# Pairing 64-row matmuls on both row halves in a fused linear-attention and gated-MLP block, with a constant in the rows for z2's shift

## The chip, the cores and the metric

One core of a Trainium2 chip runs the whole kernel. The metric is the time of one execution on the device in microseconds (us). The profiled execution also has a span, from its first to its last recorded instruction.

## The reference

All inputs are bf16; S = 2048 tokens, D = 448 features, 16 heads of 28, F/2 = 896. Part A is a linear attention with softmax features, part B a gated MLP whose gate mixes tokens. Both work on a layer norm whose scale and shift come from a condition c.

```python
mod = (silu(c) @ w_mod).reshape(1, 6, 1, 448)          # sa, ca, ga, sb, cb, gb
h = layernorm(x) * (1 + ca) + sa
q, k, v = split_heads(h @ wqkv)                        # 16 heads of 28
phi_q = concat(softmax(q @ w_phi), softmax(-(q @ w_phi)))   # phi_k likewise
o = (phi_q @ (phi_k.T @ v)) / (phi_q @ sum(phi_k) + 1e-6)
x = x + ga * (o @ wo)
h = layernorm(x) * (1 + cb) + sb
z = gelu(h @ w_in)                                     # 448 -> 1792
z1, z2 = z[..., :896], layernorm(z[..., 896:])
g = w_sp @ z2 + b_sp[:, None]                          # 2048 x 2048 over tokens
x = x + gb * ((z1 * g) @ w_out)
```

## The kernel before

The tokens lie in 16 tiles of 128. Features are cut into four chunks of 112 rows (448 = 4 x 112), each in its own slot of 128 rows, so a product over the 448 features is four matmuls of 112 rows accumulated in one PSUM bank. The layer norm's shift rides on row 113 of the first chunk: xpad holds ones behind each chunk's 112 columns (m1, L676), the transposes put them into row 112 of hT, and the weight has the shift's product there; hence KR = [113, 112, 112, 112] (L847). The scale of the norm is multiplied into the weight rows (SC, L776; SCw, L782).

The order of every engine's work is one table written out by hand, ORDER (L482). Each word is a step: its name, its arguments, after @ the PSUM slot (A0, A1, A2 are pairs of banks, B0 and B1 single banks), after / the engine (V VectorE or DVE, S ScalarE or ACT, G GpSimd or POOL, Y SyncE or SP). The steps are issued in the order of the table, so each engine runs its own steps in that order; waits between engines follow from the data and from the reuse of slots. DMA loads and transposes stand in the table too, nearly all in SP's queue (T1 and T2 through turn, L832; T3, L1007; W, L1048, which brings the token-mixing matrix transposed into four 512-column pieces, of which the last three reuse the memory of Eq and hT; ld, the loads of L639; oD, L1077).

The stages, in the order of the table:

1. Start: the condition's silu (ct, ce), loads, folding w_phi into the q and k weights (FT, ET, PF, EP, L789 to L815), the columns of shift and scale (colform, L743; col_shift, col_scale), the shift rows of q, k, v (SH, L758) and the scalings (SC). Dummy matmuls du keep TensorE at work meanwhile. The first norm is l1s, l1e, l1r, l1a; its first four tiles are transposed by TensorE (X, XE), the others by DMA (T1).
2. The k and v stage: per tile kM, kE/kF (two exponentials), kS, kR, kP, vM, vC, and kA, the sum over tokens. Half of the q units (qM:0 to 2) lie among them.
3. The numerator stage: KV and KZ build the block-diagonal matrix; qM makes the rest of the q features (each 8 matmuls of 512 columns, with two exponentials qE/qF on ACT); per tile nM (8 matmuls of 120 columns), nX (ACT copies the sums), nC, per two tiles nS (three small DVE operations: add, reciprocal, multiply, L948), nT (DVE, 896 wide), nA (adds the two halves into opad), T2 (transposes to oT), wM or wN (L966: four matmuls with the output projection; wN adds x by an identity matmul), wR (new x and its sum, ACT or DVE), wQ (its squares), l2R, l2r, l2a (second norm into xpad), T3 (transposes to hT). The shift rows of w_in are SHw (L763: four units of four matmuls of 448 columns), its scalings SCw.
4. The z stage: per tile zM (L1011: 8 matmuls of 448 columns into both banks of an A slot), zG (gelu with its sum), zQ (squares), zR and zW (moments), zN (the norm into z2n). z1 is made transposed: yM (L1040) is one of 7 x 4 units of four matmuls of 512 columns into one bank, of any slot, yG its gelu.
5. The g stage: gM (L1055: 16 matmuls over all tokens), gG (two DVE operations), oM (seven matmuls), oE, oD. Some z1 units lie among the gM here.

The core of the two products and of the output projection:

```python
def zM(i, slot):
    t = ps["z" + str(i)] = bank(slot, "z2_ps")
    for hf in range(2):
        for m in range(KC):
            nc.tensor.matmul(t[:, hf, 0:D], lhsT=hT[0:KR[m], i, m, :], rhs=win_s[0:KR[m], m, FH + hf * D:FH + (hf + 1) * D], ...)
```

The second path (general_path) runs only if a sum overflows, and does not run here; guard (L1080) is the test for it, with a one-column matmul.

Of the kernel before, what the change touches and what calls it, by code (L numbers as in the profile page):

```python
# [481 lines left out]
ORDER = """  # L482
m3 m4 m1/G m2b/V m2a/V ld:x0/Y l1s:0 ld:c/S ld:wq/S du:3@A2 ct@B0 tbl ce:1 ce:2 l1e:0,1/G l1r:0,1 l1a:0/G ce:3 ce:4 du:14@A2 FTq:0@B1 du:1@A2 FTq:1@B0
ETq:0/S X:0@A2 XE:0/S ld:wk/Y FTk:1@A1 ETk:1/S FTk:0@B1 ETk:0/S ld:phi/Y ETq:1/V bd/V scb ld:x1/Y l1s:1 l1e:1,2/G l1r:1,2 l1a:1/G PFq:3@B0 PFq:2@A2
PFq:1@A1 EPq:2/S EPq:1/S ld:x2/Y EPq:3/V l1s:2 l1s:3 l1e:2,4/G l1r:2,4 du:4@A0 PFk:0@B0 PFk:2@B1 PFq:0@A2 PFk:1@A0 ld:wsa/Y du:1@A1 csA@A1 EPk:0/S
EPk:1/S PFk:3@B0 X:1@A0 EPk:3/S XE:1/S EPk:2/S EPq:0/V esA SHq@A2 ld:wca/Y ccA@B0 l1a:3/V X:3@A1 l1a:2/V ecA SCq:0/V SCq:3/V SCq:2/V SCq:1/V X:2@A0
SHk@B0 XE:3/S XE:2/S ld:wv/Y ld:x3/Y SCk:0/S ld:x4/Y SHv@B1 SCk:2/V SCk:1/V SCv:2/V SCv:3/V l1s:4 l1s:5 l1s:6 l1s:7 l1s:8 l1s:9 l1s:10 ld:wmgb/Y
ld:x5/Y ld:wo/Y ld:wmga/Y SCv:1/S SCv:0/S l1e:4,8/G l1r:4,8 l1a:5/G l1a:4/G SCk:3/S qM:0@A2 vM:0@B0 qF:0 vC:0 qE:0 kM:0@B1 vM:1@A1 vC:1 kE:0 kM:1@B0
vM:2@A2 vM:3@A1 l1a:6/G l1a:7/G kF:0 kF:1 kE:1 vC:2 kM:2@B1 kM:3@B0 kS:0 l1s:11 kS:1 kR:0 l1e:8,12/G l1r:8,12 kP:0/V kR:1 kP:1/G l1a:9/G vC:3 kE:2
qM:1@A2 gr:1@A1 kF:3 kE:3 kF:2 ge:1 qE:1 T1:4,6 kA:0@A0 gr:0@B0 kM:4@B1 qF:1 kF:4 kE:4 kS:2 kS:3 kR:2 l1s:12 T1:6,8 ld:wout/Y qM:2@A1 kA:1@A0 kM:5@B1  # L490
kR:3 kP:2/V l1a:8/G kP:3/G kS:4 l1s:13 kR:4 kP:4/V T1:8,10 W:0,2 W:0,5 l1a:10/G wts:4/G l1a:11/G T1:10,12 ge:0 ld:wsb/S qF:2 kA:2@A0 vM:4@B0 kA:3@A0
kE:5 kF:5 kM:6@B1 l1s:14 l1s:15 l1e:12,16/G l1r:12,16 l1a:13/G vC:4 qE:2 kE:6 kF:6 kA:4@A0 vM:5@B0 kM:7@A2 kM:8@B1 vM:6@A1 kE:7 vC:5 kF:7 kS:5 kR:5
l1a:15/G l1a:14/G kP:5/V kS:6 kS:7 kR:6 kR:7 kP:6/V kP:7/V l1a:12/G T1:12,14 wos:0/G ld:win1/S kF:8 T1:14,16 W:0,0 W:0,1 ld:wcb/Y W:0,7 ld:bsp/Y W:0,4
vC:6 kA:5@A0 vM:7@B0 kM:9@A2 vM:8@A1 kE:8 kF:9 vC:7 kE:9 kA:6@A0 kM:10@B1 kE:10 kF:10 vC:8 kA:7@A0 kM:11@B0 vM:9@A2 kM:12@B1 kF:11 kE:11 W:0,3
ld:win0/Y vC:9 kS:8 kR:8 kS:9 kR:9 kP:8/G kS:10 kS:11 kR:10 kP:9/G kR:11 kP:10/V kP:11/G kA:8@A0 kE:12 kF:12 vM:10@B0 kM:13@A2 vC:10 kA:9@A0 kF:13
kE:13 kS:12 kR:12 kP:12/G kS:13 kR:13 kP:13/G vM:11@B0 vC:11 kA:10@A0 kM:14@B1 kE:14 kF:14 wts:0/G wos:1/G wts:6/G wos:2/G wts:2/G wts:1/G wos:3/G
kA:11@A0 kS:14 kR:14 kP:14/V vM:12@B0 kM:15@A2 vC:12 kF:15 kE:15 vM:13@B1 vC:13 kA:12@A0 kS:15 kR:15 kP:15/V vM:14@B0 kA:13@A0 vM:15@B1 vC:14 vC:15
kA:14@A0 csB@B0 kA:15@A0 esB KV:0/V KV:1/V KZ:0 KZ:1 qM:3@A2 ccB@B0 nM:0@A1 nM:1@A0 ecB qF:3 nX:0 SHw:3@B0 SHw:2@B1 nX:1 nC:0 nC:1 nS:0 nT:0 nA:0/V
T2:0,1 W:0,6 nT:1 SCw:3,1/G SCw:1,1/G SCw:0,2/V SCw:0,3/V SCw:2,1/V nA:1/G T2:1,2 qE:3 qM:4@A2 qM:5@A1 qF:4 qE:4 nM:2@A0 nM:3@A2 nX:2 nC:2 nX:3 nC:3
nS:1 qF:5 nT:2 nT:3 qE:5 wN:0@B0 wR:0/S SHw:1@B1 dm:9,3 nM:4@A1 nM:5@A0 SCw:0,1/S nX:4 nX:5 nC:4 nC:5 nS:2 nA:2/G nT:4 nA:3/G nT:5 nA:4/G wN:1@B0  # L500
wQ:0/S wR:1/S wQ:1/S SHw:0@B1 SCw:2,0/S l2R:0,2/G l2r:0,2 l2a:0/G SCw:0,0/V nA:5/V T2:2,4 T2:4,6 qM:6@A2 nM:6@A1 nM:7@A0 wN:2@B0 wN:3@B1 qE:6 nX:6
nC:6 nX:7 nC:7 nS:3 nT:6 nT:7 qF:6 wR:2/S wQ:2/S wR:3/S wQ:3/V l2R:2,4/V nA:6/G nA:7/G l2r:2,4 l2a:3/G l2a:2/G qM:7@A2 nM:8@A1 nM:9@A0 wN:4@B0 wM:5@B1
W:1,1 T3:0,1 T2:6,8 qE:7 nX:9 nC:9 nX:8 qF:7 zM:0@A2 wR:4/S gt zG:0 nC:8 l2a:1/V nS:4 nT:8 nT:9 T3:1,2 wR:5/V nM:10@A1 nX:10 wM:6@B0 wQ:4/V wR:6/V
SCw:1,0/G SCw:3,0/G wQ:5/S l2R:4,6/G l2r:4,6 l2a:4/G nM:11@A0 nX:11 nC:10 nC:11 zQ:0/S zM:1@A2 zG:1 zQ:1/S zR:0,2/G zW:0,2 nA:8/V nS:5 nA:9/V nT:10
T3:2,4 wM:7@B0 wR:7/V l2a:5/V W:1,5 T2:8,10 T3:4,6 yM:0,0@B1 zM:2@A2 zM:3@A1 yG:0,0 wQ:6/S zG:2 zG:3 nT:11 nM:12@A0 nM:13@A2 wQ:7/V zN:0/V zN:1/V
nX:12 wM:8@B0 wM:9@B1 nC:12 nX:13 nC:13 zQ:3/S zQ:2/S zM:4@A1 nA:10/V nS:6 wR:8/V nA:11/G nT:12 nT:13 wR:9/V nA:12/V nA:13/V l2R:6,8/G l2r:6,8 l2a:6/G
l2a:7/G T2:10,12 wQ:8/S wQ:9/V zR:2,4/G zW:2,4 yM:0,1@B0 l2R:8,10/G l2r:8,10 l2a:8/G l2a:9/G zG:4 yG:0,1 zQ:4/S zN:2/V zN:3/V zM:5@A0 nM:14@A2
nM:15@A1 wN:10@B0 wN:11@B1 zG:5 nX:14 nX:15 nC:14 nC:15 nS:7 wR:10/S wQ:10/V nT:14 nT:15 nA:14/V nA:15/V wR:11/S zQ:5/S zR:4,6/G zW:4,6 T3:6,8 zM:6@A0
zG:6 wQ:11/S zQ:6/S T2:12,14 W:1,0 wM:12@B0 wM:13@B1 zM:7@A2 l2R:10,12/V yM:0,4@A1 yM:1,4@A0 l2r:10,12 l2a:11/G T3:8,10 T2:14,16 zG:7 zQ:7/S zN:4/V
zN:5/V zR:6,8/G zW:6,8 wR:13/V yG:0,4 wQ:13/S zM:8@A2 zM:9@A1 l2a:10/V wR:12/V wM:14@B0 wM:15@B1 wQ:12/V l2R:12,14/V W:1,3 T3:10,12 W:2,1 l2r:12,14  # L510
l2a:12/G zN:6/V zN:7/V yG:1,4 zG:8 zG:9 zQ:8/S W:1,4 zM:10@A2 zM:11@A1 zQ:9/S zR:8,10/G zW:8,10 zG:10 zG:11 zQ:11/S wR:14/V l2a:13/V T3:12,14 W:2,3
W:2,7 wR:15/V wQ:14/V wQ:15/V l2R:14,16/V yM:1,2@B0 zM:12@A2 zM:13@A1 yG:1,2 zG:12 yM:1,3@B0 yM:0,2@B1 yM:2,1@A2 yM:2,5@A0 zQ:10/V zN:8/V zN:9/V
zR:10,12/V l2r:14,16 l2a:14/V l2a:15/V zG:13 zQ:13/S zW:10,12 T3:14,16 W:1,2 zN:10/V zN:11/V zQ:12/V W:2,0 W:2,6 W:1,7 W:2,5 W:2,4 W:2,2 yG:1,3 yG:2,1
zM:14@A1 zM:15@A2 yG:2,5 W:1,6 zG:14 zG:15 zQ:15/S yM:1,5@B0 yG:0,2 yM:3,0@A1 yM:0,6@A2 yM:1,1@A0 yG:3,0 yG:1,1 yG:1,5 wts:3/G zR:12,14/V zW:12,14
zN:12/V zN:13/G zQ:14/V yM:3,6@B1 yM:0,3@A1 yM:1,6@B0 yG:0,3 yG:1,6 yM:1,0@A0 yG:1,0 yG:3,6 yM:3,3@A1 yM:0,5@B0 yG:0,5 yG:3,3 yG:0,6 zR:14,16/V
zW:14,16 zN:14/G zN:15/V gM:0,6@B1 gM:0,3@B0 gG:0,3 gM:0,4@A2 gG:0,6 gM:0,2@B0 yM:2,4@B1 yM:2,6@A1 yG:2,6 yG:2,4 gG:0,4 gG:0,2 yM:3,5@A2 yM:3,1@B0
yM:2,3@B1 yG:3,5 wts:5/V yG:2,3 yG:3,1 gM:0,0@A2 gG:0,0 gM:0,5@B0 gG:0,5 yM:2,0@B1 gM:0,1@A2 gG:0,1 gM:1,4@B0 oM:0,0,7@A2 oM:3,0,7@A1 yM:3,4@A0 gG:1,4
oE:0 oM:2,0,7@B0 yM:3,2@A2 yG:3,4 yG:2,0 yG:3,2 guard@A0 gM:1,5@B1 oM:1,0,7@A2 oE:1 oE:2 oE:3 gM:1,2@A0 gG:1,2 gM:1,1@B0 gM:1,3@A2 gM:1,0@A1 gG:1,3
gG:1,0 gM:1,6@A2 oD:0/Y oD:3/Y oD:2/Y gG:1,1 gG:1,5 gG:1,6 gM:2,0@B0 yM:2,2@B1 yG:2,2 W:3,0 W:3,3 W:3,7 W:3,1 W:3,6 W:3,4 W:3,2 gM:2,2@A2 gG:2,0
# [658 lines left out]
```

## Time and profile before

| what | us |
|---|---|
| median of 3 runs (264.61 to 271.07) | 265.28 |
| the profiled execution's own time | 264.1 |
| its span | 262.2 |
| PE (TensorE) busy in it | 251.1 (96%) |
| DVE busy | 158.1 (60%) |
| ACT busy | 107.4 (41%) |
| POOL busy | 89.3 (34%) |

PE is the matmuls, PEld the weight loads, which run beside them; the granted TensorE clock is 0.997 of full speed over the span. The chain that ended last is 87% PE work. A row of a group gives line, engine, operation, output<-inputs by the program's names and sizes, count, then busy time and mean duration, then the idle time ahead of it and what ended it. Matmuls overlap, so a group's pitch (start to start) is shorter than its mean duration; the chain of waits and the timeline, with starts and merged lengths, give the pitch.

### The profile page before, as it was taken

What the parts mean: (1) busy time and instruction counts of PE and PEld (TensorE: products, weight loads), DVE (VectorE), ACT (ScalarE), POOL (GpSimd) and SP (SyncE); (2) the same over time, 40 slices, a digit from 0 to 9 for tenths busy, and PEclk for the clock granted to TensorE, in tenths of its full rate; (3) what the DMA queues carried; (4) which work ended last, traced back from release to release, by engine and by line L of the source; (5) the groups of instructions that cost most, each with busy time, mean ns of one, the idle gap of its engine ahead of it and who ended that gap; (6) DMA issues with size and microseconds to landing.
All of it is one profiled execution on the core that took longest, in us unless ns stands there. A gap on an engine that the chain in (4) does not pass through costs nothing.

```text
span 262.2 us, 4353 instructions
## 1 busy us (share of the span) xinstructions
PE 251.1 (96%) x1639; PEld 135.6 (52%) x1648; DVE 158.1 (60%) x359; ACT 107.4 (41%) x222; POOL 89.3 (34%) x149
## 2 busy tenths in 40 slices
...
GB/s 187 265 287 118 215 224 207 225 159 54 66 103 126 98 118 131 171 131 173 162 0 2 1 0 0 20 2 75 0 2 143 157 0 0 20 105 2 0 38 61
DMA packets 68655, 25.23 MB, mean 96 GB/s; under 512 B 58129, under 2 KB 68498, under 8 KB 68626
## 3 DMA queue, kind: packets, MB, share of 16 engines
...
HBM read 8.87 MB, written 1.84 MB: 41 GB/s over the span
## 4 chain that ended last, share of the span: by engine, by line
PE 87%; DVE 7%; DMA 2%; issue 1%; POOL 1%; ACT 0%; ACTq 0%; DVEq 0%; POOLq 0%
PE g_ps L1059 37%; PE z_ps L1043 9%; PE z_ps L1015 9%; PE o_ps L1072 8%; PE k_ps L852 4%; PE v_ps L860 4%; PE q_ps L907 3%; PE x_ps L971 3%; DVE f_t L955 3%; PE kvacc L883 3%; DMA f_wq_raw<-in_A_wqkv_dram 2%; PE num L935 2%; PE sh_ps L761 1%; PE pf_ps L811 1%; DVE f_w L952 1%
## 5 line engine op out<-in xcount | busy, mean ns | idle before, releaser
L1059 PEld LDWEIGHTS <-f_z2n 128*128 128x128 bf16 x560 | 50.2, 98 | 46.9
L1065 DVE TENSOR_TENSOR f_gb<-g_ps,f_bsp 128x512 f32<-128x512 f32 (+2 forms) x35 | 20.4, 583 | 55.9 <-PE g_ps L1059 53.7
L1059 PE MATMUL g_ps<-f_Eq,f_z2n 128*128 128x512 bf16 x218 | 49.0, 379 | 0.3
L1046 ACT ACTIVATE f_z1T<-z_ps 128x512 bf16<-128x512 f32 x28 | 15.6, 592 | 61.8 <-PE z_ps L1043 61.7
L1015 PE MATMUL z_ps<-f_win,f_hT 112*128 112x448 bf16 (+1 forms) x128 | 26.1, 352 | 0.0
L1043 PE MATMUL z_ps<-f_hT,f_win 113*128 113x512 bf16 (+1 forms) x112 | 26.1, 379 | 0.0
L1059 PE MATMUL g_ps<-f_hT,f_z2n 128*128 128x384 bf16 (+1 forms) x224 | 25.1, 272 | 0.0
L1059 PE MATMUL g_ps<-f_wsp,f_z2n 128*128 128x512 bf16 x109 | 24.5, 379 | 0.2
L1072 PE MATMUL o_ps<-f_wout,f_z1T 128*128 128x448 bf16 x112 | 23.0, 352 | 0.1
L1075 DVE TENSOR_TENSOR f_xpad<-o_ps,f_x 128x448 bf16<-128x448 f32 x16 | 9.6, 620 | 20.7 <-PE o_ps L1072 20.7
L1066 DVE TENSOR_TENSOR f_z1T<-f_gb,f_z1T 128x512 bf16<-128x512 f32 (+2 forms) x35 | 20.5, 585 | 1.5
L1015 PEld LDWEIGHTS <-f_hT 112*128 112x128 bf16 (+1 forms) x128 | 12.4, 97 | 12.0 <-DMA f_hT<-f_xpad 0.4
L912 ACT ACTIVATE f_Eq<-q_ps 112x1024 bf16<-112x1024 f32 x16 | 16.1, 1030 | 5.6 <-PE q_ps L907 5.6
L1043 PEld LDWEIGHTS <-f_win 113*128 113x128 bf16 (+1 forms) x112 | 10.9, 97 | 13.0
L855 ACT ACTIVATE f_E<-k_ps 128x448 bf16<-128x448 f32 x32 | 15.9, 550 | 4.1 <-PE k_ps L852 2.5
L866 DVE TENSOR_REDUCE f_ksum<-f_E 128x32 f32<-128x896 bf16 x16 | 16.7, 1060 | 0.8 <-ACT f_E L855 0.8
L955 DVE TENSOR_TENSOR f_t<-num,f_w 128x896 bf16<-128x896 f32 x16 | 16.8, 1084 | 0.4
L1019 ACT ACTIVATE f_z2g<-z_ps 128x896 bf16<-128x896 f32 x16 | 14.7, 916 | 3.8 <-PE z_ps L1015 3.6
L1072 PEld LDWEIGHTS <-f_z1T 128*128 128x128 bf16 x112 | 10.9, 98 | 10.1
L907 PE MATMUL q_ps<-f_hT,f_Wq 113*128 113x512 bf16 (+1 forms) x64 | 15.2, 379 | 0.6 <-DVE f_t L955 0.6
L860 PE MATMUL v_ps<-f_wv,f_hT 113*128 113x448 bf16 (+1 forms) x64 | 14.6, 352 | 0.0
L852 PE MATMUL k_ps<-f_Wk,f_hT 113*128 113x448 bf16 (+1 forms) x64 | 14.5, 352 | 0.0
...
## 6 DMA issues: line engine op xcount, KB each, us to landing
...
```

Source lines behind the costliest of these rows:

```text
L852: nc.tensor.matmul(t[:, 0, 0:D], lhsT=hT[0:KR[m], i, m, :], rhs=Wk[0:KR[m], m, :], start=(m == 0), stop=(m == KC - 1))
L860: nc.tensor.matmul(t[:, 0, 0:D], lhsT=hT[0:KR[m], i, m, :], rhs=wv[0:KR[m], m, :], start=(m == 0), stop=(m == KC - 1))
L866: nc.vector.tensor_reduce(out=ksum[:, i], in_=Er[i % NR][:].rearrange("p s (c f h) -> p (s c) h f", c=4, h=HP), axis=AX.X, op=ALU.add)
L907: nc.tensor.matmul(t[:, u, :], lhsT=Wq[0:KR[m], m, cc * CB:cc * CB + P], rhs=hT[0:KR[m], 4 * st:4 * st + 4, m, :], start=(m == 0), stop=(m ...
L912: nc.scalar.activation(out=Eq[st // 2][0:CB, 2 * c2:2 * c2 + 2, s, (st % 2) * 512:(st % 2 + 1) * 512], in_=ps["q" + str(n)][0:CB, :, :], f ...
L955: nc.vector.tensor_tensor(out=tr[i % 2][:], in0=numv(i)[:, :, :, 0:DH], in1=wr[i // 2 % 2][:, i % 2].unsqueeze(3).to_broadcast([P, 2, H, D ...
L1015: nc.tensor.matmul(t[:, hf, 0:D], lhsT=hT[0:KR[m], i, m, :], rhs=win_s[0:KR[m], m, FH + hf * D:FH + (hf + 1) * D], start=(m == 0), stop=(m ...
L1043: nc.tensor.matmul(t[:, 0, :], lhsT=win_s[0:KR[m], m, fc * P:(fc + 1) * P], rhs=hT[0:KR[m], 4 * st:4 * st + 4, m, :], start=(m == 0), stop ...
L1059: nc.tensor.matmul(g[:, 0, 0:b - a], lhsT=later["z2n"][:, s_, fc * P:(fc + 1) * P], rhs=wspT[t][:, s_, a:b], start=(s_ == 0), stop=(s_ == ...
L1065: nc.vector.tensor_tensor(out=gb, in0=ps["G%d_%d" % (ch, fc)][:, 0, 0:b - a], in1=bsp[:, t * TCHF + a:t * TCHF + b], op=ALU.add)
L1066: nc.vector.tensor_tensor(out=z, in0=gb, in1=z, op=ALU.mult)
L1072: nc.tensor.matmul(ps["o" + str(t)][:, 0, 0:D], lhsT=later["z1T"][:, fc, t * P:(t + 1) * P], rhs=wout_s[:, fc, :], start=(fc == 0), stop=( ...
```

## The change

The rows are cut anew for w_in, the output projection and what is multiplied with them: windows of 128 rows that begin at rows 0, 128, 192 and 320. Windows 0, 1 and 3 are full; of window 2 only its upper 64 rows are used (rows 256 to 319). So 448 rows are seven halves of 64. A unit with two banks then takes, for each bank, seven 64-row matmuls; PAIRS puts them in pairs, one on the lower row half for one bank and one on the upper half for the other bank. In part one (four pairs) the lower half writes bank 0 and the upper half bank 1; in part two (three pairs) it is the other way round. Part two's first matmuls wait for a no-op on SP (zP, yP, wP), which waits for part one's last matmul. Other work of PE stands between the parts in the table.

- z2 (zM, zB) and z1 (yM, yB; now 14 units of 1024 columns in an A slot, with one gelu each) are done in pairs, and so is the output projection of tiles 8 to 15, two tiles at a time (wS, wM/wN, wB/wC). Tiles 0 to 7 keep one bank and whole matmuls (wU, wV): windows 0, 1 and 3 with 128 rows, window 2 with 64.
- The ones behind the chunks are gone from the second norm. l2a now adds a constant: x times rstd plus (mean term + 0.125), with l2t making that number per tile. z2's shift then is one row vector added to all scaled weights (SHu: 8 matmuls of 448 columns, uC, SCu: a tensor-by-tensor addition of 128 x 896); z1's shift is a bias of its gelu (SHz: 28 one-column matmuls, SBz). SHw and esB are gone, eg1, eg2 and gB are new.
- nA and l2a write 512 columns (the windows overlap) instead of 448. w_in and wo are loaded as windows in two loads each, so there are three more loads.
- nS is split into nD, nI and nS, so that other steps can stand between. dm's dummies are no longer in the table.
- The table is new throughout: at the start k's weights are folded ahead of q's, wq is loaded through SP; all z1 units stand before the first gM; zQ is 8 times on ACT (13 before), nA four times on POOL (7 before).

```diff
+SHIFT = 0.125
+PAIRS = [((0, 0, 0), (1, 1, 0)), ((0, 0, 1), (1, 1, 1)), ((0, 0, 2), (1, 1, 2)), ((0, 0, 3), (1, 1, 3)),
+         ((1, 0, 0), (0, 1, 0)), ((1, 0, 1), (0, 1, 2)), ((1, 0, 3), (0, 1, 3))]
+def wins(v):
+    return bass.AP(tensor=v.tensor, offset=v.offset, ap=[list(v.ap[0]), [192, 2], [1, 256]])
...
+m1/V m3 m4 ld:c/S m2a/V du:3@A2 ct@B0 tbl ce:1 ld:x0/Y ld:x2/Y ce:2 ce:3 ce:4 scb ld:wk/Y ld:x1/Y ld:phi/Y du:14@A2 FTk:1@B0 ETk:1/S FTk:0@B1 l1s:0
...
+nX:13 nA:10/V nC:12 nC:13 nD:6 l2t:5/V nI:6 nS:6 l2t:4/V gt wQ:6/S nA:11/G nT:12 nT:13 l2t:3/G l2a:3/G l2a:4/G l2a:5/G wS:8@B0 zM:0@A1 wM:8@B1 zP:0
+zB:0 wP:8 wB:8 wR:8/V wR:9/V nA:12/V zG:0 wQ:7/S l2R:6,8/G l2r:6,8 l2t:6/G l2t:7/G l2a:6/G zQ:0/S T2:10,12 zM:1@A0 nM:14@A1 nM:15@A2 nX:14 nX:15 nC:14
+nC:15 nA:13/V nD:7 nI:7 nS:7 nT:14 nT:15 T3:2,4 zP:1 zB:1 T3:4,6 zG:1 wQ:8/S zQ:1/S zR:0,2/G zW:0,2 wQ:9/S l2a:7/V l2R:8,10/V W:2,3 wS:10@B0 wN:10@B1
+wP:10 zM:2@A0 zP:2 wC:10 zB:2 zG:2 zM:3@A1 zM:4@A2 zM:5@A0 T2:12,14 wR:11/S wR:10/S wQ:11/S W:1,2 zP:3 zP:4 T3:6,8 zB:3 wS:12@B0 zB:4 zQ:2/V zN:0/V
...
+    def load_wins(eng, j, dst, src):
+        eng.dma_start(out=dst[:, 2 * j:2 * j + 2], in_=src[192 * j:192 * j + 256].rearrange("(k p) n -> p k n", p=P))
...
+    W4 = [0, 128, 192, 320]
+    ROWS = [slice(0, P), slice(0, P), slice(64, P), slice(0, P)]
+    HALF = [slice(0, 64), slice(64, P)]
+    def eg1(eng):
+        eng.tensor_scalar(out=tneg[:], in0=cb1[:], scalar1=-1.0 / D, scalar2=None, op0=ALU.mult)
+    def eg2():
+        nc.vector.scalar_tensor_tensor(out=g4[:], in0=ps["csB"][:, 0, 0:KC], scalar=1.0 / (D * SHIFT), in1=tneg[:], op0=ALU.mult, op1=ALU.add)
+    def gB(eng):
+        copy_on(eng, Gb[:], g4[:].unsqueeze(2).to_broadcast([P, KC, P]))
...
-    def SHw(n, slot):
-        t = ps["SHw" + str(n)] = bank(slot, "sh_ps")
+    def SHu(h, slot):
+        t = ps["SHu" + str(h)] = bank(slot, "su_ps")
         for m in range(KC):
-            nc.tensor.matmul(t[:, 0, 0:D], lhsT=Gb[0:CB, m, :], rhs=win_s[0:CB, m, n * D:(n + 1) * D], start=(m == 0), stop=(m == KC - 1))
+            nc.tensor.matmul(t[:, 0, 0:D], lhsT=Gb[ROWS[m], m, :], rhs=win_s[ROWS[m], m, FH + h * D:FH + (h + 1) * D], start=(m == 0), stop=(m == KC - 1))
+    def SCu(m, eng):
+        v = win_s[:, m, FH:2 * FH]
+        eng.tensor_tensor(out=v, in0=v, in1=ub[:].rearrange("p a d -> p (a d)"), op=ALU.add)
+    def SHz(slot):
+        t = ps["SHz"] = bank(slot, "sz_ps")
+        for fc in range(FC):
+            for m in range(KC):
+                nc.tensor.matmul(t[:, 0, fc:fc + 1], lhsT=win_s[ROWS[m], m, fc * P:(fc + 1) * P], rhs=g4[ROWS[m], m:m + 1], start=(m == 0), stop=(m == KC - 1))
...
+    def sP(key):
+        n = passed[key] = nc.sync.nop()
+        tc.add_manual_dep(n.ins, first[key].ins.name, SYNC, reason="part one of the unit")
+    def pairs(part, key, dst, lhs, rhs, extra=()):
+        steps = list(extra) + [[(bk, lhs(bk, HALF[hf], m), rhs(bk, HALF[hf], m)) for bk, hf, m in pr_] for pr_ in (PAIRS[:4] if part == 0 else PAIRS[4:])]
+        for n, st_ in enumerate(steps):
+            for bk, l, r in st_:
+                ins = nc.tensor.matmul(dst[bk], lhsT=l, rhs=r, start=(part == 0 and n == 0), stop=(part == 1 and n == len(steps) - 1))
+                if part == 0:
+                    first[key] = ins
+                elif n == 0:
+                    tc.add_manual_dep(ins.ins, passed[key].ins.name, SYNC, reason="the other row half writes this bank next")
...
-            nc.tensor.matmul(t[:, 0, 0:D], lhsT=oT[0:CB, i % 4, cc, :], rhs=wo_s[0:CB, cc, :], start=(cc == 0 and not with_x), stop=(cc == KC - 1))
+        for n, m in enumerate((0, 1, 3, 2)):
+            nc.tensor.matmul(t[:, 0, 0:D], lhsT=oT[ROWS[m], i % 4, m, :], rhs=wo_s[ROWS[m], m, :], start=(n == 0 and not with_x), stop=(n == KC - 1))
...
+    def l2t(i, eng):
+        eng.tensor_scalar(out=nt2[:, i:i + 1], in0=m2[:, i:i + 1], scalar1=v2[:, i:i + 1], scalar2=SHIFT, op0=ALU.mult, op1=ALU.add)
...
+    def zM(i, part, slot=None):
+        if part == 0:
+            ps["z" + str(i)] = bank(slot, "z2_ps")
+        t = ps["z" + str(i)]
+        pairs(part, "z%d" % i, [t[:, bk, 0:D] for bk in range(2)], lambda bk, r, m: hT[r, i, m, :], lambda bk, r, m: win_s[r, m, FH + bk * D:FH + (bk + 1) * D])
...
+    def yG(sp, fc):
+        nc.scalar.activation(out=stage_b()["z1T"][:, fc, sp * 1024:(sp + 1) * 1024], in_=ps["y%d_%d" % (sp, fc)][:].rearrange("p a d -> p (a d)"), func=ACT.Gelu_apprx_tanh,
+                             bias=zb1[:, fc:fc + 1])
```

190 lines of the change are left out of this document (104 added, 86 removed).

## The prediction, made before the changed kernel ran

> **What bounds the kernel now.** I read the page's busy times first, then the busy time by stretch, then what TensorE (PE) waited for, then the chain that ended last. The first line is the page's, the next seven are the stretches that the later steps use: the start, the k and v stage, the numerator stage up to the first z2 product, the z2 stage, the last z1 units ahead of the gate (g) products, and the two halves of the g stage.
>
> ```profile
> PE 251.1 (96%) x1639; PEld 135.6 (52%) x1648; DVE 158.1 (60%) x359; ACT 107.4 (41%) x222; POOL 89.3 (34%) x149
> ```
> ```profile
> 0.00:15.50 15.50, 12.63 (x152) 9.43 (x153) 10.03 (x37) 9.34 (x17) 7.34 (x27) 1.00 0.97 240
> 15.50:54.60 39.10, 38.73 (x306) 22.57 (x305) 36.49 (x70) 30.92 (x60) 31.78 (x33) 1.00 1.03 206
> 54.60:79.25 24.65, 22.36 (x190) 12.78 (x189) 20.83 (x48) 16.75 (x37) 15.57 (x21) 1.00 0.37 83
> 79.25:122.80 43.55, 42.97 (x256) 22.55 (x256) 37.57 (x109) 37.52 (x86) 32.58 (x68) 1.00 0.71 134
> 122.80:131.50 8.70, 8.70 (x42) 3.88 (x40) 1.84 (x7) 6.39 (x12) 2.01 (x2) 1.00 0.93 164
> 131.50:175.00 43.50, 43.29 (x202) 19.90 (x205) 13.46 (x23) 5.92 (x11) 0.00 (x0) 1.00 0.01 4
> 175.00:257.70 82.70, 82.40 (x500) 44.44 (x502) 37.24 (x68) 0.60 (x1) 0.00 (x0) 1.00 0.20 43
> ```
> ```profile
> PE num L940 <- DVE f_t L955: 1.6, 1, 1.6
> ```
>
> The columns of a stretch are its length and the busy time of PE, its weight loads, DVE, ACT and POOL, then the granted clock (1.00), the DMA share and GB/s. PE is the bound almost everywhere: from 79.25 to 257.70 it idles about 1 us in 178. Only in the numerator stage (54.60 to 79.25) it idles 24.65 - 22.36 = 2.3 us, and PE's longest wait, 1.6 us, is for DVE's f_t (nT). So a matmul taken away after 79 us is worth its pitch; one taken away before is worth it only if DVE and ACT allow it. In the z2 stage DVE and ACT are each busy 37.5 us of 43.55, 86%: little room once PE is shortened.
>
> **The change part by part.** The pitches are from the chain of waits (start, length, what).
>
> ```profile
> 56.34 0.38 PE cf_ps L747 x16
> ...
> 67.72 0.39 PE num L940 x9
> 68.11 0.85 PE num L935 x16
> 68.95 0.19 PE x_ps L969
> 69.14 0.76 PE x_ps L971 x4
> 69.91 0.76 PE sh_ps L766 x4
> 70.66 1.75 PE q_ps L907 x8
> ...
> 104.78 3.04 PE z_ps L1015 x16
> ...
> 122.81 8.68 PE z_ps L1043 x40
> ```
>
> A 512-column matmul takes 8.68/40 = 0.217 us, a 448-column one 3.04/16 = 0.190, a one-column one 0.38/16 = 0.024. If the two halves of a pair run side by side, a pair costs one pitch:
> - z1: 28 units x 4 = 112 matmuls become 14 units x 7 = 98 pairs: -14 x 0.217 = -3.0.
> - z2: 16 x 8 = 128 become 16 x 7 = 112 pairs: -16 x 0.190 = -3.0.
> - output projection of tiles 8 to 15: 32 become 28 pairs, -0.8; but the identity product runs nine times instead of seven, +0.4.
> - shift rows: 16 SHw matmuls go (-3.0), 8 SHu come (+1.5), 28 one-column SHz come (28 x 0.024 = +0.7).
> - The nine dummies of dm go: 0.39 us inside a wait for nT, so nothing.
>
> Together -7.2 us of PE work: 6.8 behind the first z2 product, where PE is the bound, and 0.4 ahead of it.
>
> **Switching between full height and half height.** SHz and SHu hold a 64-row matmul among 128-row ones for each of 7 + 2 units, wU/wV for 8 tiles (17 x 2 = 34 switches), and the pair stage is entered and left twice (4). The trace has no 64-row matmul. Its nearest row is the one-column matmul of the guard, a change of the array's shape in width.
>
> ```profile
> 169.00 1.03 PE L1043 MATMUL z_ps<-f_hT,f_win 113*128 113x512 bf16 x4
> 169.96 0.16 PE L1086 MATMUL fl_ps<-f_ones,f_flb 128*1 128x1 bf16 x1
> 170.06 1.04 PE L1059 MATMUL g_ps<-f_Eq,f_z2n 128*128 128x512 bf16 x4
> ```
> ```profile
> 169.96 0.08 PEld L1086 LDWEIGHTS <-f_flb 128*1 128x1 bf16 x1 [0.42 <-issue]
> ```
>
> The four z1 matmuls should stream 4 x 0.217 = 0.87 us, to 169.87; the guard's load starts only at 169.96, and the next full one 0.10 after it, where the pitch would be 0.024. So in and out cost (0.19 - 0.02)/2, about 0.08 us a switch. Bounds: 0, and 0.10. I take 0.08: 34 x 0.08 = 2.7 us ahead of the z2 products and 0.3 behind. [...]
>
> **The numerator stage.** From the end of the k stage (54.60) to the first z2 product PE now has five qM (5 x 1.75), fourteen nM (14 x 0.425), two colforms (0.76), SHz and SHu (2.2), and wV/wU for eight tiles (7.4): 25.0, with switches 27.7 us. DVE's chain has, per pair of tiles, from nC to the end of the second nT:
>
> ```profile
> 73.57 0.30 DVE f_cr L946 x2
> ...
> 74.83 2.09 DVE f_t L955 x2
> ```
>
> 73.57 to 76.92, 3.35 us. nM:13 needs nT:10, five and a half pairs: 18.4. DVE's other work in today's stretch is 7.4 (20.83 less the four pairs in it); six more nA and SCu:2 come, three SCw, wQ:3 and l2R:2,4 go, and I leave it at 7.4. With about 2 us until the first numerators have been drawn out that is 27.8, beside PE's own 27.7, and each waits for the other at every pair. Walking both engines' orders tile by tile with these durations I get the first z2 product 29.7 us behind the k stage: 2.0 us of PE idle, as the 2.3 now. The bounds are 27.7 and 32.0 (twice the idle). ACT nearly fills the stretch too: some 26 us, an estimate from the two ACT rows of the z stage by columns (ten qE and three scalings at about 1.0, seven wR and seven wQ at about 0.6, nX, gB, uC and the table load). POOL gets three SCu (128x896, tensor by tensor) and three SCs:
>
> ```profile
> L873 POOL TENSOR_TENSOR f_phik<-f_E,f_kr 128x896 bf16<-128x896 bf16 x7 | 11.9, 1710 | 2.6 <-PE k_ps L852 2.6
> ```
>
> At 1.7 us each at most 10.3, covered: between SHu and the first z2 product PE has some 20 us of qM, nM and wV. Without that cover it would cost up to 10.
>
> **Start.** Now k is folded first. The first full-height product behind the folding is kM:0, which waits for ACT's two SCk, behind two ETk, four EPk, four EPq and three XE.
>
> ```profile
> 8.49 1.73 ACT L799 COPY f_wTk<-tps 112x896 bf16<-112x896 bf16 x2
> 10.08 1.00 ACT L799 CAST f_Wq<-pf_ps 112x448 bf16<-112x448 f32 x2
> ```
> ```profile
> 15.48 1.90 PE L907 MATMUL q_ps<-f_hT,f_Wq 113*128 113x512 bf16 x8
> ```
>
> 1.73 + 13 x 0.5 = 8.2 us, begun when wk has landed (now about 7.2, as for wq), gives 15.4 if ACT never waits; with waits between folds and copies I take 16.3. PE now becomes dense at 15.48: +0.9. Bounds: -0.1, and +2.8 if wv, now queued behind x3 as well, holds SHv (448 KB at the 240 GB/s of the first stretch are 1.9 us more). csB moves out of the k stage, -0.4. The k stage then ends at 55.1.
>
> **The z stage.** From the first z2 product to g: z2 112 x 0.190 = 21.3, z1 98 x 0.217 = 21.3, wM 5.7, nM:14 and 15 0.85, switches 0.3: 49.4. ACT up to zG:15:
>
> ```profile
> L1019 ACT ACTIVATE f_z2g<-z_ps 128x896 bf16<-128x896 f32 x16 | 14.7, 916 | 3.8 <-PE z_ps L1015 3.6
> L983 ACT ACTIVATE f_junk<-f_z2g 128x896 bf16<-128x896 bf16 x13 | 12.4, 950 | 0.3
> ```
>
> 16 zG at 1.0 (with the accumulator's read), 8 zQ at 0.95, five yG at 1.0 (1024 wide, from 0.92 for 896), eight wQ and wR at 0.6 (448 wide): 33 us against PE's 35.6 there. PE still bounds, barely. Every two-bank unit now needs one of the three A slots, which nM:14 and 15 use too, and the z1 fillers no longer fit the single banks. I give 2.0 us of new idle, bounds 0.6 (the z2 stretch now, 43.55 - 42.97) and 2.3 (the numerator stretch); nearest the latter, since DVE and ACT are filled alike.
>
> Each unit's second part waits for a no-op on SP, queued with the transposes:
>
> ```profile
> 115.97 1.23 SPq L1009 DMA_TRANSPOSE f_hT<-f_xpad  x1
> 117.25 11.05 SPq L1051 DMA_TRANSPOSE f_Eq<-in_B_w_sp_dram  x8
> ```
> ```profile
> SPq L834 <- DVE f_opad L961: 8.0, 4, 3.3
> ```
>
> A transpose holds SP 1.23 to 1.38 us, and one may wait 3.3 us for nA. In the new table nearly every second part stands behind 0.9 to 3.6 us of other PE work, with at most two transposes ahead of its no-op (zP:3 behind T2:12,14 and W:1,2, 2.6 us, against 3.6). So 0 beyond the 2.0; upper end, 34 no-ops each behind a transpose, 34 x 1.3 = 44.
>
> **The sum.** 55.1 + 29.7 + 49.4 + 2.0 = 136.2: g starts, with no z1 unit left. Now g starts at 131.5 and PE ends at 257.70, with nine z1 units (9 x 4 x 0.217 = 7.8) between: 126.2 - 7.8 = 118.4. PE ends at 254.6; the last stores end 4.5 later, as now (262.2 - 257.7): 259.1. The profiled execution took 264.1 for its span of 262.2, so 1.9 lies around it: **261.0 us**, 3.1 below its own time. The median of the runs is 265.28, 1.2 above the profiled one; a measurement of this kernel can tell about 2% from no change.
>
> **The rivals.**
> 1. The halves don't hide their weight loads (the other side). If a half's load had to wait until the matmul on the same rows has streamed, each of the 240 pairs (112 + 98 + 30) would add what the guard's load showed, 0.09: 21.6 us, 282.6. It cancels the gain from 3.1/240 = 0.013 us a pair, and is over 2% slower from (270.6 - 261.0)/240 = 0.04. Against it:
>
> ```profile
> 83.08 1.29 PEld L1015 LDWEIGHTS <-f_hT 113*128 113x128 bf16 x8
> ```
> ```profile
> 83.13 1.69 PE L1015 MATMUL z_ps<-f_win,f_hT 113*128 113x448 bf16 x8
> ```
> The eight loads of a z2 unit run under its matmuls, though all use the same rows. For it: no half-height load is in the trace. [...] Chance 12%.
>
> 2. SP. A third of the no-ops come 0.7 us late, behind a transpose that itself waits: 11 x 0.7 = 8, 269.0. For it: the 3.3 us wait. Against: the spacing above. Chance 15%.
>
> 3. The whole PE cut shows: the switches are free (-1.7: the 0.3 and half of the 2.7, since DVE holds the other half), no new idle in the z stage (-2.0), no later start (-0.9): 256.4. For it: PE idles only 0.6 us in today's z2 stage with the same fill. Chance 25%.
>
> **How the numbers follow.** My forecast has 45%, with its own range 257.5 to 264.5 (below, half of the switches and the idle's 0.6; above, the start's +2.8 and a little); 3% stay for a start that goes wrong. Faster by over 2% (under 260.0): rival 3 and a third of mine, 0.40. Slower by over 2% (over 270.6): rival 1, a third of rival 2 and a little, 0.18. Within 2%: 0.42. The range 254.5 to 270 leaves out rival 1, the far part of rival 2 and the end of rival 3.
>
> **What would show it.** Pairs: z2's 14 matmuls within 7 x 0.19 + 0.1 us; loads under them. Switches: a gap of about 0.08 around each 64-row matmul of wV. Numerator stage: PE waits for f_t, about 2 us in all. SP: PE's second parts waiting for SP, under 1 us in all. PE busy by about 244 us. A pair pitch over 0.23 us, waits for SP above 3 us, or a first z2 product after 88 us would make the prediction wrong.

## The result, and the profile after

| | before | after |
|---|---|---|
| median of 4 runs each (us) | 265.04 | 275.01 |
| lowest, highest | 264.61, 271.07 | 274.16, 278.19 |
| the profiled execution | 264.1 | 274.78 |
| its span | 262.2 | 273.0 |
| its granted clock | 0.997 | 0.978 |

The changed kernel is slower: 1.040 of the time before, 95% interval 1.031 to 1.048. The forecast was 261.0 us, the range ended at 270.0. Some executions run at a lower granted clock and take over 1.5% longer (the kernel before in the round of e1: 268.56 to 271.79 us at 0.984 to 0.991, the others 264.12 to 265.72 us at 0.994 to 1.000; by its time 271.07 us is one too); the ratios leave them out, and of e4_before_guard below the profiled execution is one, with a wait of 6.9 us in the k stage, so only its g stage is read.

The page's busy line and its TensorE clock in 40 slices, then the stretches of after between the same events as in the prediction: PE dense, end of the k and v stage, first z2 product, last z1 units, g, and two parts of the g stage (columns as there).

```profile
PE 253.3 (93%) x1867; PEld 134.9 (49%) x1875; DVE 162.8 (60%) x362; ACT 109.7 (40%) x218; POOL 101.9 (37%) x155
PEclk9999999997999999999999995999999999999998
```
```profile
0.00:16.70 16.70, 13.65 (x159) 10.30 (x160) 11.35 (x38) 10.21 (x20) 8.74 (x29) 1.00 0.98 242
16.70:56.14 39.44, 38.70 (x290) 21.83 (x289) 36.03 (x62) 30.12 (x59) 33.13 (x33) 1.00 1.01 211
56.14:89.50 33.36, 30.25 (x259) 16.02 (x258) 28.33 (x64) 24.75 (x60) 23.87 (x35) 0.95 0.48 95
89.50:127.94 38.44, 36.74 (x371) 17.95 (x372) 32.04 (x95) 32.37 (x68) 31.37 (x57) 1.00 0.78 139
127.94:141.65 13.71, 13.71 (x129) 7.26 (x125) 4.24 (x14) 10.68 (x14) 4.79 (x4) 1.00 0.21 39
141.65:180.00 38.35, 33.25 (x144) 14.73 (x146) 11.15 (x19) 1.57 (x2) 0.00 (x0) 0.91 0.26 43
```

The reader is to see two holes in a clock that was at 1.00 in all seven stretches of the kernel before: slice 10 (61 to 68 us) and slice 25 (164 to 171 us). And PE, 93% busy, idles 5.1 us of the 38.35 at the start of g, where it idled 0.2 of 43.50 before. By stage, in us:

| stage | before | forecast | after | after - forecast |
|---|---|---|---|---|
| to the end of the k and v stage | 54.60 | 55.1 | 56.14 | +1.0 |
| numerator stage, to the first z2 product | 24.65 | 29.7 | 33.36 | +3.7 |
| z stage, to the start of g | 52.07 | 51.4 | 52.15 | +0.8 |
| g stage, to the end of PE | 126.4 | 118.4 | 125.65 | +7.2 |
| tail | 4.5 | 4.5 | 5.7 | +1.2 |

(Before, nine z1 units lie in the g stage.) The sum of the last column is 13.9 = 273.0 - 259.1. So the z stage, for which the change was made, came out nearly as forecast; two others did not.

**The g stage.** What PE waited for longest in after, then PE's timeline from the first g unit, then two stretches with their granted clock:

```profile
PE fl_ps L1180 <- DVE f_flb L1178: 4.5, 1, 4.5
PE num L1007 <- DVE f_t L1032: 2.1, 2, 1.9
...
PE z_ps L855 <- SPq L847: 0.6, 1, 0.6
...
PE x_ps L855 <- SPq L847: 0.3, 1, 0.3
```
```profile
141.65 20.89 PE L1153 MATMUL g_ps<-f_wsp,f_z2n 128*128 128x512 bf16 x94
167.08 0.16 PE L1180 MATMUL fl_ps<-f_ones,f_flb 128*1 128x1 bf16 x1 [4.54 <-DVE f_flb L1178]
167.48 1.87 PE L1153 MATMUL g_ps<-f_wsp,f_z2n 128*128 128x512 bf16 x4 [0.24 <-DVE flag L1181]
169.56 3.73 PE L1153 MATMUL g_ps<-f_wsp,f_z2n 128*128 128x512 bf16 x11 [0.22 <-issue]
173.13 10.52 PE L1153 MATMUL g_ps<-f_Eq,f_z2n 128*128 128x512 bf16 x47
```
```profile
165.15:168.56 3.41, 1.24 (x4) 0.59 (x5) 2.98 (x8) 0.00 (x0) 0.00 (x0) 0.50 0.00 0
168.56:171.97 3.41, 3.19 (x8) 1.21 (x8) 1.56 (x3) 0.00 (x0) 0.00 (x0) 0.50 0.03 10
```

The longest wait is for the guard, the test for overflow, which is no part of the pairs. In the old table it stands behind oE:0 and several z1 units, and its matmul at 169.96 waited for nothing. The new table puts it behind gG:0,2. So PE stands at the one-column matmul while DVE does two gG (2.8 us) and the guard's two reductions (0.59 and 0.60), and then the sixteen matmuls of gM:0,3 (15 of them are in the trace) take 5.65 us, up to 173.13, where they should take 16 x 0.217 = 3.47, because the clock is halved until 171.97 (the 0.50 of the last two rows). From the end of the g units (162.54) to 173.13 10.6 us pass with 3.5 us of work in them: 7.1 us lost, 2.2 of them to the clock.

**The numerator stage.** PE there, from the second colform on:

```profile
60.07 0.58 PE L1007 MATMUL num<-f_KVbd,f_Eq 112*128 112x120 bf16 x8 [0.52 <-ACT f_Eq L984]
60.49 2.01 PE L816 MATMUL sz_ps<-f_g,f_win 128*128 128x1 bf16 x28
62.36 0.64 PE L1007 MATMUL num<-f_KVbd,f_Eq 112*128 112x120 bf16 x8
62.79 3.57 PE L803 MATMUL su_ps<-f_win,f_Gb 128*128 128x448 bf16 x8
66.20 1.90 PE L979 MATMUL q_ps<-f_hT,f_Wq 113*128 113x512 bf16 x8
```
```profile
59.33:62.75 3.42, 2.90 (x53) 2.60 (x51) 3.04 (x9) 1.39 (x3) 1.35 (x2) 1.00 0.00 0
62.75:66.16 3.41, 3.41 (x12) 0.82 (x10) 2.70 (x6) 2.38 (x5) 1.01 (x2) 0.50 0.38 77
```

SHz takes 62.36 - 60.49 = 1.87 us; 28 x 0.024 = 0.67 was its work, and 14 changes of height account for the rest at 0.086 each. Then the eight SHu take 3.41 us, where 1.52 and four changes of height would be 1.9 (and are 1.94 in e3 below): the second fence shows the clock at 0.50 for exactly 3.41 us. So at first sight the stage lost 1.2 us by heights, which the forecast had counted (14 of its 34 switches), and 1.5 by the clock, which it had not. The experiments showed that this reading is not the whole.

**The z stage.** Its pairs, the last stretch of each kind:

```profile
123.36 4.76 PE L855 MATMUL z_ps<-f_win,f_hT 64*128 64x448 bf16 x48
127.94 13.78 PE L855 MATMUL z_ps<-f_hT,f_win 64*128 64x512 bf16 x126
```

48 z2 matmuls, 24 pairs, start 4.58 us ahead of the next row: 0.191 us a pair. 126 z1 matmuls, 63 pairs, fill 13.71 us up to g: 0.217 a pair, one pitch, though each half has its own load (0.094 us).

### The profile page after: what moved, and what is told of

It is laid out like the page before. It is cut to its first block, busy times and chain, and to the rows that moved or that the text cites. A ratio compares the mean times of both kernels' runs of the same rounds, so it can differ in the third digit from the quotient of the medians.

```text
span 273.0 us, 4860 instructions
## 1 busy us (share of the span) xinstructions
PE 253.3 (93%) x1867; PEld 134.9 (49%) x1875; DVE 162.8 (60%) x362; ACT 109.7 (40%) x218; POOL 101.9 (37%) x155
## 4 chain that ended last, share of the span: by engine, by line
PE 78%; DVE 9%; POOL 3%; DMA 3%; ACT 2%; issue 2%; SPq 0%; POOLq 0%; DVEq 0%; ACTq 0%
PE g_ps L1153 36%; PE z_ps L855 11%; PE o_ps L1166 8%; PE q_ps L979 5%; PE k_ps L924 4%; PE v_ps L932 4%; PE kvacc L955 2%; DMA f_wk_raw<-in_A_wqkv_dram 2%; DVE f_t L1032 2%; PE x_ps L1060 1%; DMA f_hT<-f_xpad 1%; PE num L1007 1%; PE su_ps L803 1%; ACT f_Eq L984 1%; DVE f_dn L1022 1%
## 5 line engine op out<-in xcount | busy, mean ns | idle before, releaser
L1153 PE MATMUL g_ps<-f_wsp,f_z2n 128*128 128x512 bf16 x109 | 26.4, 401 | 0.6 <-DVE flag L1181 0.2
L855 PE MATMUL z_ps<-f_win,f_hT 64*128 64x448 bf16 x224 | 24.1, 350 | 1.9 <-DVE f_t L1032 0.8
L855 PE MATMUL z_ps<-f_hT,f_win 64*128 64x512 bf16 x196 | 22.6, 376 | 0.0
L855 PEld LDWEIGHTS <-f_hT 64*128 64x128 bf16 x224 | 10.8, 94 | 13.5 <-DMA f_hT<-f_xpad 1.8
L1139 ACT ACTIVATE f_z1T<-z_ps,f_zb 128x1024 bf16<-128x1024 f32 x14 | 15.3, 1111 | 3.7 <-PE z_ps L855 3.5
L855 PEld LDWEIGHTS <-f_win 64*128 64x128 bf16 x196 | 10.8, 94 | 9.9 <-SPq L847 0.3
```

Source lines behind the costliest of these rows:

```text
L855: ins = nc.tensor.matmul(dst[bk], lhsT=l, rhs=r, start=(part == 0 and n == 0), stop=(part == 1 and n == len(steps) - 1))
L1153: nc.tensor.matmul(g[:, 0, 0:b - a], lhsT=later["z2n"][:, s_, fc * P:(fc + 1) * P], rhs=wspT[t][:, s_, a:b], start=(s_ == 0), stop=(s_ == ...
```

## The experiments

All times are compared through their ratio to the kernel before, measured beside each of them. PE's stage lengths in one profiled execution each (us), with the ratio of the times:

| kernel | numerators | z | g | ratio to before (95%) |
|---|---|---|---|---|
| after | 33.36 | 52.15 | 125.65 | 1.040 (1.031 to 1.048) |
| e1_guard_late | 34.66 | 51.87 | 119.76 | 1.016 (1.011 to 1.021) |
| e3_both | 36.81 | 51.58 | 119.77 | 1.022 (1.014 to 1.030) |
| e10_scu_only | 34.38 | 52.37 | 119.77 | 1.015 (1.008 to 1.023) |
| e5_scu_dve | 31.49 | 52.88 | 119.77 | 1.013 (1.010 to 1.016) |
| e6_no_scu_pool | 30.46 | 52.29 | 119.76 | 1.006 (1.004 to 1.007) |
| e8_merge | 30.80 | 51.81 | 119.76 | 1.008 (1.005 to 1.011) |
| e9_all | 30.14 | 52.08 | 118.54 | 1.000 (0.997 to 1.002) |
| e7_whole | 33.48 | 57.36 | 119.75 | 1.039 (1.036 to 1.042) |
| e11_start | 30.70 | 52.17 | 118.53 | 1.015 (1.011 to 1.020) |

### The guard: e1 and e4

```diff
-gG:0,0 gG:0,2 guard@B0 gG:0,5 gG:0,4 gM:0,3@B0 gM:1,2@A2 gG:0,3 gM:1,1@B1 gM:1,4@B0
+gG:0,0 gG:0,2 gG:0,5 gG:0,4 gM:0,3@B0 gM:1,2@A2 gG:0,3 gM:1,1@B1 guard@B0 gM:1,4@B0
```

> The changed kernel with the guard moved back behind three more g units (after gM:1,1), nothing else. Theory (the moved guard): in the changed kernel PE waits 4.5 us for flb and then runs four matmuls in 1.87 us instead of 0.87 because the clock halves after the wait; with the reductions under gM:0,3, gM:1,2 and gM:1,1 both go, the guard's matmul waits under 0.3 us, the granted clock stays at 1.00 through the g stage, and the time falls by 6.0 to 6.5 us, to about 268.7 us. Rival (the clock falls by itself, because the pairs load the array more densely): the clock still shows two half-speed windows in the g stage, only the wait goes, and the time falls by 4 to 4.5 us or less, to 270.5 us or more.

Measured 269.53 us, nearer the theory's 268.7 than the rival's 270.5. PE at the guard now:

```profile
164.55 3.61 PE L1153 MATMUL g_ps<-f_wsp,f_z2n 128*128 128x512 bf16 x16 [0.78 <-DVE f_gb L1159]
168.00 7.07 PE L1153 MATMUL g_ps<-f_Eq,f_z2n 128*128 128x512 bf16 x32
175.00 0.16 PE L1180 MATMUL fl_ps<-f_ones,f_flb 128*1 128x1 bf16 x1
175.40 3.61 PE L1153 MATMUL g_ps<-f_Eq,f_z2n 128*128 128x512 bf16 x16 [0.23 <-DVE flag L1181]
```

The matmul waits for nothing, the clock stays full in the g stage (1.00 from 141 to 264 us), and that stage is 5.9 us shorter. The rival falls: with the same pairs ahead of it the clock is not halved there. What is left, 0.78 and 0.23 us, is the slot B0, which gM:0,3 and gM:1,4 take right behind its last user.

The opposite edit, the guard of the kernel before moved to the start of g (the diff is one word moved, from behind yG:3,2 to right behind gG:0,3, and its slot, B0 for A0; so one gG stands ahead of it, not two as in the changed kernel and in the text below):

> The kernel before with only its guard moved to the place that it has in the changed one: behind the first two products of the gate (after gG:0,3 and gG:0,6). Theory (the place of the guard is what costs): PE waits about 4 us for flb, the clock halves for one or two windows of 3.4 us, and the time rises by 4.5 to 6.5 us, to about 270.5 us. Rival (the wait is dear only in the changed kernel, with its pairs and its order): under 2 us more, below 267 us.

The median of all its runs is 273.27 us; the ratio is 1.024 (1.017 to 1.032), some 6.5 us. Its guard:

```profile
153.85 0.16 PE L1086 MATMUL fl_ps<-f_ones,f_flb 128*1 128x1 bf16 x1 [3.15 <-DVE f_flb L1084]
153.95 8.41 PE L1059 MATMUL g_ps<-f_wsp,f_z2n 128*128 128x512 bf16 x32
162.19 2.98 PE L1043 MATMUL z_ps<-f_hT,f_win 113*128 113x512 bf16 x13
```

3.15 us of waiting, then 32 matmuls in 8.24 us up to the next row instead of 6.94: 1.3 us for the clock (granted 0.50 from 153.26 to 156.67). The g stage is 4.5 us longer, 130.9 against 126.4. So one word of the table costs both kernels about 2%, and the price has nothing to do with the pairs.

### SHz: e2 and e3

```diff
-        for fc in range(FC):
-            for m in range(KC):
+        for m in (0, 1, 3, 2):
+            for fc in range(FC):
...
```

> The changed kernel with SHz's loops exchanged: the 21 one-column matmuls on 128 rows first, then the 7 on 64 rows, so 2 changes of height instead of 14. Theory (changes of height, and the clock that falls after 1.9 us of sparse work): SHz takes about 0.85 us instead of 1.87 (12 changes at 0.09), the clock window behind it is full again, SHu takes 1.5 us instead of 3.41, the first z2 product comes about 2.9 us earlier and the time is about 272 us. Rival (the clock falls for another reason, such as the two short idles around csB and the numerators): SHu stays at 3.4 us, only 1.0 us is gained and DVE's chain may take even that, 274 to 275 us.

Measured 276.21 us, ratio 1.039 (1.031 to 1.047): nothing gained. With the late guard:

> Both edits, the guard behind gM:1,1 and SHz with its 64-row matmuls together. Theory: the two losses lie in different stages and add, 6.3 + 2.9 = 9.2 us, so about 265.8 us, equal to the kernel before within 1%; PE busy about 247 us. Rival (the clock falls by itself): at most 4.5 + 1.0 us, 269.5 us or more.

Measured 271.83 us: at most e1's gain and none of SHz's, so the theory is wrong in its second half. Yet SHz did what it should. PE of e3_both:

```profile
60.94 0.93 PE L816 MATMUL sz_ps<-f_g,f_win 128*128 128x1 bf16 x28
61.84 0.58 PE L1008 MATMUL num<-f_KVbd,f_Eq 112*128 112x120 bf16 x8
62.25 2.10 PE L803 MATMUL su_ps<-f_win,f_Gb 128*128 128x448 bf16 x8
...
74.53 0.98 PE L1008 MATMUL num<-f_KVbd,f_Eq 112*128 112x120 bf16 x8 [3.71 <-DVE f_t L1033]
```

SHz takes 0.90 us and SHu 1.94 (its work and four changes of height); but from 70.8 to 74.5 PE waits 3.71 us for DVE's f_t where it waited 1.9, and then the clock halves there, for two windows (0.50 from 73.85 to 80.68). DVE and POOL (GpSimd) of the same kernel ahead of that wait:

```profile
64.60 0.65 DVE L1030 TENSOR_TENSOR f_w<-f_Sx,f_dn 128x64 f32<-128x64 f32 x1
65.35 2.09 DVE L1033 TENSOR_TENSOR f_t<-num,f_w 128x896 bf16<-128x896 f32 x2
67.36 3.07 DVE L1039 TENSOR_TENSOR f_opad<-f_t 128x512 bf16<-128x512 bf16 x2
70.35 0.28 DVE L1019 TENSOR_TENSOR f_cr<-num,f_Sx 128x32 f32<-128x32 f32 x2
70.66 0.68 DVE L1023 TENSOR_TENSOR f_dn<-f_cr 128x32 f32<-128x32 f32 x1
71.38 0.35 DVE L1026 RECIPROCAL f_dn<-f_dn 128x32 f32<-128x32 f32 x1
71.77 1.58 DVE L1030 TENSOR_TENSOR f_w<-f_Sx,f_dn 128x64 f32<-128x64 f32 x1
```
```profile
66.25 3.90 POOL L810 TENSOR_TENSOR f_win<-f_win,f_ub 128x896 bf16<-128x896 bf16 x2
70.13 1.18 POOL L829 TENSOR_SCALAR f_win<-f_win,f_cb 128x896 bf16<-128x896 bf16 x1
71.39 1.87 POOL L810 TENSOR_TENSOR f_win<-f_win,f_ub 128x896 bf16<-128x896 bf16 x1
```

This is the find of the study. f_w is 64 numbers wide and takes 0.22 us elsewhere (at 76.81); here 1.58, and it ends at 73.35, just behind POOL's SCu (71.39 + 1.87 = 73.26). f_opad takes 0.42 alone (at 76.95); two take 3.07 and end behind the pair of SCu that ends at 70.15. Operations with one operand in PSUM or with one operand at all keep their times beside SCu: f_t with 2.09 us for two and f_cr with 0.28 for two in after (at 72.39 and 74.39, an SCu from 73.35 to 75.23), the reciprocal with 0.35 here (at 71.38). In e10_scu_only, which has no SCu on POOL, they take the same 2.09, 0.28 and 0.35 (at 72.16, 74.17 and 74.93). So here DVE's operations on two SBUF operands, f_w and f_opad, stood until POOL's addition was through.

It is not the additions alone. The f_w of 0.65 us stands beside POOL's scalings (64.17 to 66.17), and the trace before had such a row already, which ends behind the first of two scalings:

```profile
59.28 1.01 DVE L952 TENSOR_TENSOR f_w<-f_Sx,f_dn 128x64 f32<-128x64 f32 x1
```
```profile
59.20 2.01 POOL L772 TENSOR_SCALAR f_win<-f_win,f_cb 112x896 bf16<-112x896 bf16 x2 [0.40 <-PE sh_ps L766]
```

In after f_dn and f_w are held ahead of PE's wait of 1.86 us, which ends at 73.53: beside two of POOL's SCu, from 68.56 to 72.27, they take 0.7 and 1.2 us longer than alone (0.19 and 0.22 in e3_both, at 75.99 and 76.81), together as much as that wait:

```profile
69.59 0.90 DVE L1022 TENSOR_TENSOR f_dn<-f_cr 128x32 f32<-128x32 f32 x1
...
70.91 1.45 DVE L1029 TENSOR_TENSOR f_w<-f_Sx,f_dn 128x64 f32<-128x64 f32 x1
```

### SCu away from POOL: e5, e6, e10

```diff
-SCu:0/G SCu:1/G ... SCu:3/G
+SCu:0/V SCu:1/V ... SCu:3/V
```

> The kernel of e3_both with the three SCu on GpSimd (the additions of the shift row to the z2 weights, 1.88 us each) moved to DVE, at the same places of the table. Theory (POOL's additions hold up those operations of DVE that read two operands from SBUF): f_dn and f_w, which took up to 1.16 and 1.57 us beside SCu, and f_opad (3.07 us for two) return to 0.23, 0.23 and 0.41 us each; DVE takes on 3 x 0.62 = 1.85 us, and gets back about 5; PE's wait of 3.7 us for f_t falls under 1.5 us, so that the clock does not halve behind it (1.9 us more); time 266 to 268 us. Rival (DVE's chain is simply full, and the long durations come from something else): f_dn and f_w stay long, DVE is later by 1.85 us, time 273 us or more.

> The kernel of e3_both without the three SCu on GpSimd: the shift row is added to one of the four windows only, so z2 lacks most of its shift; everything else is done. Theory (POOL's additions hold up DVE): as with SCu on DVE but 1.85 us of DVE work less, PE's longest wait for f_t under 1 us, time 265 to 267 us. Rival (the long DVE durations come from something else, such as DMA transposes at 170 to 190 GB/s in that stretch): within 1 us of the 271.8 us of e3_both.

Measured 267.88 and 265.53 us: as the theory said, at the end of its range and within it. DVE in e5_scu_dve, the same operations and the additions:

```profile
66.90 0.75 DVE L1039 TENSOR_TENSOR f_opad<-f_t 128x512 bf16<-128x512 bf16 x2
...
68.72 0.22 DVE L1030 TENSOR_TENSOR f_w<-f_Sx,f_dn 128x64 f32<-128x64 f32 x1
...
76.18 2.83 DVE L810 TENSOR_TENSOR f_win<-f_win,f_ub 128x896 bf16<-128x896 bf16 x3
```

DVE does three additions itself in 2.83 us (one takes 0.62, at 75.27; about 1.0 of the 2.83 is spent beside two operations of POOL, l2a at 75.51 and a scaling at 76.72) and is earlier all the same. The numerator stage is 5.3 us shorter than in e3_both, 6.3 without the additions; no clock window is halved in e5 (granted 1.00 up to 141 us), so e3's two are in the 5.3. By the ratios e5 gains 0.9%, with intervals that overlap, and e6 1.7%, clear of e3_both. One f_dn, which the text above puts down to SCu, keeps its 1.16 us in e5: it stands at 62.55 beside POOL's two nA (61.40 to 63.66), and with those on DVE (e9) it takes 0.19.

The fourth corner, the old SHz with SCu on DVE:

> The kernel of e1_guard_late (old SHz) with the three SCu on DVE: the fourth corner of the square of SHz (old, new) and SCu (GpSimd, DVE). Theory (both SHz's changes of height and POOL's additions cost, and the first was hidden in e3_both by the second): against e5_scu_dve, which differs only by SHz, SHz takes 1.9 us instead of 0.9 and the clock halves behind it, so 1.0 to 2.9 us slower than e5_scu_dve's 267.9, that is 269 to 271 us; against e1_guard_late's 269.5 between 1 us slower and 1.5 us faster. Rival (SHz never mattered, only POOL's additions): equal to e5_scu_dve, 267.9 us.

Measured 269.69 us, ratio 1.015: inside the theory's range, with a stage of 34.38 us against e5's 31.49. So neither edit gains alone (34.66 to 36.81 and to 34.38) and both together gain 3.2. Behind the held DVE a fast SHz was of no use: PE waited for f_t instead. Behind the slow SHz, PE's wait of 1.58 us for f_t in e1 is gone in e10, but as much comes elsewhere: 1.40 us for DVE's f_x, which stands behind the additions now, and, by PE's pitch, a second halved window right behind the first, in which a qM takes 2.73 us instead of 1.75. The times alone would not show it, for e1, e10 and e5 overlap in their intervals; the stage lengths are of one execution each, and up to two halved windows (1.7 us each) fall or don't fall into them.

### The changes of height: e8

```diff
-        for n, m in enumerate((0, 1, 3, 2)):
+        order = ["x", 0, 1, 3, 2] if i in (0, 2, 4, 6) else [2, "x", 0, 1, 3]
...
```

> The kernel of e5_scu_dve, and in addition the 64-row matmuls of neighbouring units put side by side (SHu:1 and SHu:0, and tiles 0 and 1, 4 and 5, 6 and 7 of the output projection): the second unit begins with its 64-row matmul, so 8 changes of height less. Theory (each change costs 0.09 us on PE, and PE is late there): 0.7 us below e5_scu_dve. Rival (DVE bounds the numerator stage): PE waits 0.7 us longer for f_t instead, and the time is within 0.3 us of e5_scu_dve.

Measured 266.17 us against 267.88, numerators 30.80 against 31.49: 0.69 us for eight changes, 0.086 each, in the stage. The time fell by 1.7 us; the rest lies in the z stage and the tail, which differ by 1.1 and 0.3 in the two profiled executions, and the edit does not touch them.

### The pairs: e7

```diff
-        steps = list(extra) + [[(bk, lhs(bk, HALF[hf], m), rhs(bk, HALF[hf], m)) for bk, hf, m in pr_] for pr_ in (PAIRS[:4] if part == 0 else PAIRS[4:])]
+        steps = [[(bk, ident[:], r) for bk, r in extra]] if extra else []
+        steps += [[(part, lhs(part, ALL, m), rhs(part, ALL, m))] for m in range(KC)]
```

> The kernel of e1_guard_late without pairs: each bank of z2, z1 and the output projections of tiles 8 to 15 gets four matmuls on 128 rows, first bank 0, then bank 1, with the same no-ops and the same table; window 2 is taken with all its rows, so 64 rows count twice in the sums. Theory (a pair costs one pitch): 14 x 0.217 + 16 x 0.190 + 4 x 0.190 = 6.8 us of PE work more, all where PE is the bound, so 275 to 276 us against 269.5. Rival (the pairs save less than they seem to, because ACT and DVE bound the z stage with them): 2 to 4 us more, 271.5 to 273.5 us.

Measured 274.32 us, ratio 1.039 against e1's 1.016, 2.3% or 6.1 us (4.8 by the medians), between the two but near the theory. The z stage is 57.36 against 51.87, 5.5 us longer; the numerators are 1.2 us shorter, with one halved window where e1 has two (granted 0.94 and 0.88 from 62 to 90 us). So the pairs are worth some 5.5 of the 6.8 us that I counted for them.

### All together: e9, and a start that does not fit: e11

```diff
-nA:0/G nA:1/G ... wU:3@B1 wR:3/V ... gM:0,3@B0 ... gM:1,4@B0
+nA:0/V nA:1/V ... wV:3@B1 wR:3/S ... gM:0,3@A1 ... gM:1,4@A0
...
-oE:13 oE:14 oE:15 oD:12/Y oD:10/Y oD:9/Y oD:13/Y oD:11/Y oD:14/Y oD:15/Y
+oE:13 oE:14 oE:15 oD:13/Y oD:14/Y oD:15/Y
```

> The kernel of e8_merge with four small moves: gM:0,3 takes slot A1 and gM:1,4 slot A0 (PE waits 0.78 us for f_gb and 0.24 us for the flag there now), nA:0 and nA:1 go to DVE (on GpSimd they hold f_dn for 0.97 us and f_w for 0.4), tile 3's new x is made by ACT with its identity product on PE (PE waits 0.86 us for DVE's f_x there), and the stores of tiles 9 to 12 are issued ahead of the last two g units (the span ends 5.4 us after PE now, 4.5 in the kernel before). Theory: 1.1 + 0.6 + 0.7 + 0.8 = 3.2 us less than the 266.2 us of e8_merge, 263 us, equal to the kernel before or 0.5% faster. Rival (DVE is full from 59 to 89 us, and what PE does not wait for here it waits for later): only 1.1 + 0.8 us are gained, 264.3 us.

Measured 265.06 us, ratio 1.000 (0.997 to 1.002): equal to the kernel before, but above the theory's 263 and the rival's 264.3. The g stage is one run of matmuls, its two waits gone:

```profile
139.60 24.35 PE L1156 MATMUL g_ps<-f_wsp,f_z2n 128*128 128x512 bf16 x112
163.78 7.07 PE L1156 MATMUL g_ps<-f_Eq,f_z2n 128*128 128x512 bf16 x32
170.78 0.16 PE L1183 MATMUL fl_ps<-f_ones,f_flb 128*1 128x1 bf16 x1
```

It takes 118.54 us, where 118.4 was forecast, and the numerators 30.14, where 29.7 was. The tail is still 5.5 us (263.6 - 258.14): moving stores gained nothing there. And its k stage ended at 57.38, 0.8 to 1.3 us later than in the other kernels with the same start.

e11_start puts the start of the kernel before (107 words of its table, up to the scaling SCk:3) ahead of e9's table:

> The kernel of e9_all with the start of the kernel before: the table's words up to the scalings of q, k and v (q folded ahead of k, wq loaded through ACT's queue, qM:0 as the first full-height unit) come from the kernel before, the rest in its own order. Theory (the new start is what delays the k stage): PE becomes dense at 15.5 us instead of 16.7 to 18.0, the k stage ends 1.0 to 1.4 us earlier and the time is about 263.8 us, 0.4% below the kernel before. Rival (the k and v stage is bound by DVE, ACT and GpSimd, which begin no earlier): under 0.4 us gained, 264.7 to 265.1 us.

Measured 269.02 us, 1.015 (1.011 to 1.020): worse than both said. PE's two longest waits, 1.5 us for POOL's f_phik and 1.4 us (in two) for the transposes to hT, lie in the k stage. By these waits the old start's norms and the new order of the k stage don't meet: its k stage ended at 59.54, 2.2 us later than e9's. It tells nothing for or against the new start, so the +1.0 of that stage stays open, as does the tail's.

## Why the prediction was wrong

- **Step that failed first: the g stage, "126.2 - 7.8 = 118.4".** I took the rest of the g stage as unmoved and subtracted the z1 units that left it. The new table also moves the guard, five small DVE operations and a matmul, from behind other work to the front of g, and I never looked at it. The stage is over by 7.2 us, and 7.1 are lost at the guard: e1 gets 5.9 of them back, e9 the rest by its slots, and e4 pays 4.5 in the kernel before, with one gG less ahead of the guard. Without this step the changed kernel would still have been slower than forecast, but inside the range: 269.53 (e1).
- **Step that failed second: "At 1.7 us each at most 10.3, covered".** I named as cover of POOL's additions some 20 us of PE work. That cover was there (POOL was in time), but I asked only who waits for POOL, not whom POOL holds: it held DVE by 1.9 us in after, and PE waits for DVE in this stage. With the additions off POOL the stage is 5.3 us shorter behind a fast SHz (e3 to e5, halved windows included) and 0.3 behind the slow one (e1 to e10).
- **The clock was missing.** All pitches were full-speed ones. Halved windows cost 1.5 us behind SHz and 2.2 at the guard. So the numerator stage's 3.7 are 1.5 of clock, 1.1 of idle time (3.1 us, with the wait of 1.86 in it, where 2.0 were forecast) and 1.1 of PE work that is not broken down.
- **Right:** the price of a change of height (0.08 foreseen, 0.086 by SHz and by e8); the late point "a first z2 product after 88 us would make the prediction wrong" (89.50). That a change of height costs what the change of width did, from which I took it, no row of the kernel before could tell. The numerators' 29.7 comes near what they take when little is held up (30.46 in e6, 30.14 in e9), but with 12 and 20 changes of height fewer than it counts; with all 34 it would be some 2 us too low.
- **Open:** the k and v stage came out 1.0 us later than forecast and the tail 1.2 us longer; e11 and the stores in e9 did not settle either. PE's busy time, forecast at about 244 us, is 253.3, and still 250.0 in e5 with no halved window; no run breaks this down.
- **Two slips that change little:** g starts at 131.32 in the trace before, not at 131.5, so the g stage would be 118.6; and half of the switches (1.5) and the idle's 0.6 (1.4 less) put my own range's lower end at 258.1, not 257.5.
- **The rivals:** half-height loads are hidden (pairs at 0.191 and 0.217 us, with two loads of 0.094 us each), so rival 1 is out. Waits for SP in the z stage are 0.6 + 0.3 us, under the 1 us that I gave, so rival 2 is out. The pairs' part of rival 3's cut was there (some 5.5 us by e7) and was spent elsewhere.
- **The change's own balance** is e9 against the kernel before, with the losses that I found taken out: z and g stages 170.6 us against 178.5, 7.9 less; the numerator stage, which now prepares the pairs with SHu, SHz, heights and additions, 30.14 against 24.65, 5.5 more; the k stage 2.8 and the tail 1.0 more. What is gained behind the first z2 product is spent ahead of it.
